# Weight conversion in a fused recurrence and feed-forward kernel: raw words fetched one unit ahead, conversion queued behind copies, masks and products, three prefix sums moved

## The chip, the core and the metric

The kernel runs on one core of one Trainium2 chip. The metric is the device time of one execution in microseconds (us). Every number below comes from the kernel's profile, from its trace or from the list of its times. The engines are named as the profile names them: PE is the matrix engine, PEld its weight loads, DVE the vector engine, ACT the scalar engine, POOL the general one, and SP the engine whose queue issues most transfers. Each engine works through its own list of instructions in order.

## The reference

Two blocks run one after the other. The first is a gated linear recurrence over 768 positions for 4 batches and 8 heads of width 48; the second is a product of two linear maps, followed by two more linear maps.

```python
# q, k, v, alpha: (4, 8, 768, 48) float32
for t in range(S):
    state = alpha[:, :, t, :, None] * state + np.einsum('bhd,bhe->bhde', k[:, :, t], v[:, :, t])
    y[:, :, t] = np.einsum('bhd,bhde->bhe', q[:, :, t], state)
x = y.transpose(0, 2, 1, 3).reshape(3072, 384)
a = x @ w1            # 384 x 1024, handed over as float64
b = x @ w2            # 384 x 1024
h = (a * b) @ w3      # 1024 x 1024
out = h @ w_out       # 1024 x 384
```

## The kernel before, in words

**Two parts share the engines.** Part one is the recurrence. It is cut into 24 steps (`N = 24`), each a chunk of 128 positions of one batch; six chunks make a batch. Part two is the feed-forward. Its matrix products run on float32 split into pieces (`h`, `l`, `m`), which is why one product of a 128x384 block takes nine matmuls for a contraction of 384 (L420: six in `products` with parts 0 and 1, then three with part 2). The products of `w1` and `w2` with `x` are called gates. They start inside part one, as filler, as soon as a group of three chunks has been written out and read back transposed.

**One step n of the loop at L599** traces its work in this order:

- the stores of the output chunk of two steps ago and the loads of chunks ahead, all on the SP queue (`store`, `load_v`, `load_a`, `load_kq`);
- `attend_state(n-1)` (L384 on PE: the state's share of the output), `scores(n)` (L364 on PE, then two masks `ms`, L367 on DVE), `transposed(n+1)` (L324 on PE, then two copies `qkT`, L326 on ACT);
- in every fourth step from 6 on `split_x` (L412 on ACT, L413 and L414 on DVE), which cuts a group of three chunks into pieces for the gates;
- a first piece of weight conversion (L627);
- `advance` (the decayed state, POOL), `attend(n-1)` (L390 on PE and the copies `x`, L394 on ACT), `outer(n)` (L336 on PE, then `T` on DVE), `third` (L232 and L233 on PE, L234 on ACT), a piece of gate work (`run`);
- a second piece of conversion (L636), `decayed(n+2)` (L302 on DVE: the products `qk` of keys and queries with the exponentials `e`), `logs(n+4)` (L271 on ACT: the logarithm `la` of a loaded alpha chunk `ac`), a third piece of conversion (L642), gate work, `decays(n+3)` (the prefix sum of `la` on PE, L286, or L289 from chunk 10 on, then two exponentials `e` on ACT, L292 and L293), a last piece of conversion (L646), gate work.

**Conversion** turns the float64 weights into float32 with bit operations. The weights `w1` and `w2` make twelve units of 128x512 values. A unit is a generator. Its first call issues the load of its raw 64-bit words (L192). After that it has four steps:

- step 1: ACT `rest` (L200), DVE `mant` and `power` (L201, L204), ACT `power` (L205);
- step 2: DVE L207, L208 and L210;
- step 3: ACT `w` (L217);
- step 4: DVE L219, and L221 for units 6 to 11. Units 0 to 5 leave that piece to `third` instead.

Units 0 to 5 make the first half of the gate weights, which all gates started in part one need. Units 6 to 11 are needed by the gates that follow part one. `convert(steps, ahead)` advances the oldest unit that has begun, one step per count, and before each step it issues loads until `ahead` units have begun. The pool of raw words has four buffers, `mant` three, `rest` and `power` two each.

**The order of instructions** is the tracing order only as a priority. The compiler's list scheduler places an instruction on its engine as early as it believes the inputs and buffers are there. An unmarked piece of conversion can so land in an engine's list several steps ahead of where it was traced. `after_marks(names)` opens a block in which every instruction traced on the engine of a marked instruction is listed behind it on that engine. It has no effect on other engines: `("qkT", n)` marks an ACT copy, `("ms", n)`, `("qk", n)` and `"x3"` mark DVE instructions.

**The decay of a carried state** crosses chunks in pairs. For an even chunk n inside a batch three rows (the last `e` of chunk n-1, the first `e` and the first alpha of chunk n) go to memory (L278, L295, L297, issued on POOL), come back as single values per partition (L310), and are multiplied into the state (L353 to L355) before `attend_state(n)`, which is traced in step n+1.

**After part one** only products, the conversion of `w3` and `w_out`, and the projections are left.

Of the kernel before, what the change touches and what calls it, by code (L numbers as in the profile page):

```python
# [48 lines left out]
def kernel(  # L49
# [18 lines left out]
    N = B * NCH  # L68
# [34 lines left out]
    def bank():  # L103
        return ps.tile([C, 512], FP32, tag="bank", name="bank")
# [3 lines left out]
    def after_marks(*names):  # L108
        stack = ExitStack()
        for x in names:  # L110
            stack.enter_context(tc.issue_after(mark[x]))
        return stack
# [16 lines left out]
    def load_a(n):  # L129
        if n < N:  # L130
            st["a", n] = inp.tile([C, H, D], FP32, tag="ac", name="ac")
            nc.sync.dma_start(out=st["a", n], in_=rows(alpha, n))  # L132

    def load_kq(n):
        if n >= N:
            return
        st["kq", n] = inp.tile([C, 2, H, D], FP32, tag="kq", name="kq")
        nc.sync.dma_start(out=st["kq", n][:, 0], in_=rows(k, n))  # L138
        nc.sync.dma_start(out=st["kq", n][:, 1], in_=rows(q, n))  # L139

    def load_v(n):
        if n < N:
            st["v", n] = vs[n % len(vs)]
            nc.sync.dma_start(out=st["v", n][:, :, 0:D], in_=rows(v, n))
# [91 lines left out]
    def fetch(ahead=3):  # L236
        while weights and len(begun) < ahead:
            begun.append(weights.popleft())
            next(begun[-1])

    def convert(steps, ahead=3):

        for _ in range(steps):
            fetch(ahead)
            if not begun:
                return
            x = begun.popleft()
            try:
                next(x)
                begun.appendleft(x)  # L250
            except StopIteration:
                pass
# [4 lines left out]
    def store():  # L257

        while later:
            dst, src = later.popleft()  # L260
            nc.sync.dma_start(out=dst, in_=src)
# [18 lines left out]
    def decays(n):  # L280
        if n >= N:
            return
        lc = bank()[:, 0:DM]
        la = st.pop(("la", n))
        if n < LATE:
            nc.tensor.matmul(lc, sums[:, n % 2].bitcast(FP32), la, start=True, stop=True)  # L286
        else:
            for i in range(2):
                nc.tensor.matmul(lc, sums[:, n % 2], la[:, i], start=(i == 0), stop=(i == 1))  # L289

        e = st["e", n] = work.tile([C, 2, DM], FP32, tag="e", name="e", bufs=3)
        nc.scalar.activation(e[:, 0], lc, AF.Exp, scale=-1.0)  # L292
        mark["e", n] = nc.scalar.activation(e[:, 1], lc, AF.Exp).ins  # L293
        if n in ends:
            nc.gpsimd.dma_start(out=ends[n][0:1], in_=e[0:1, 0])  # L295
        if n + 1 in ends:
            nc.gpsimd.dma_start(out=ends[n + 1][1:2], in_=e[C - 1:C, 1])  # L297
        load_ends(n)
# [6 lines left out]
    def load_ends(n):  # L305
        if n not in ends:
            return
        with nc.allow_non_contiguous_dma(reason="single values to partitions"):
            for i in range(2):
                nc.gpsimd.dma_start(out=decs[n // 2 % 2][ds(DP * i, D)].rearrange("d m j -> d (m j)"),  # L310
                                    in_=ends[n].rearrange("m (j i d) -> i d (m j)", i=2, d=D)[i])

    def transposed(n):
        if n >= N:
            return
        qk = qks[n % 3]
        qkT = work.tile([C, 2, NP, C], FP32, tag="qkT", name="qkT")

        tp = [bank().rearrange("p (i j c) -> p i j c", i=2, j=NP) for _ in range(2)]
        for i in range(2):  # L320
            for j in range(NP):
                for half in range(2):
                    s = ds(DP * half, DP)
                    nc.tensor.transpose(tp[half][:, i, j, :], qk[s, i, 2 * j:2 * j + 2, :], ident[s, s])  # L324
        for half in range(2):
            mark["qkT", n] = nc.scalar.copy(qkT[:, :, :, ds(DP * half, DP)], tp[half]).ins  # L326
        st["qkT", n] = qkT
# [30 lines left out]
    def scores(n):  # L358
        qkT = st["qkT", n]
        sc = [bank().rearrange("p (j c) -> p j c", j=NP) for _ in range(2)]  # L360
        for j in range(NP):
            for i in range(2):
                r = ds(DP * i, D)
                nc.tensor.matmul(sc[i][:, j, :], qkT[r, 0, j, :], qkT[r, 1, j, :], start=True, stop=True)  # L364
        ms = work.tile([C, 2, NP, C], FP32, tag="ms", name="ms")
        for i in range(2):
            masked = nc.vector.tensor_tensor(ms[:, i].bitcast(I32), sc[i].bitcast(I32), keep_bc, op=ALU.bitwise_and)  # L367
        ends_of_part1[0] = mark["ms", n] = masked.ins
        st["ms", n] = ms
# [3 lines left out]
    def attend_state(n):  # L373
        qkT = st.pop(("qkT", n))

        y = [bank()[:, 0:HP * C].rearrange("p (j c) -> p j c", c=C) for _ in range(2)]
        st["y", n] = y, [(half * HP + j, i, y[i][ds(DP * half, DP), j, :])
                         for j in range(HP) for i in range(2) for half in range(2)]  # L380
        if n % NCH:
            for j, i, to in st["y", n][1]:
                r = ds(DP * i, D)
                nc.tensor.matmul(to, Ts[n % 2][r, j, :], qkT[r, 1, j, :],  # L384
                                 start=(j % HP == 0), stop=False, skip_group_check=True)
# [18 lines left out]
    def load_x(g, queue=nc.sync):  # L404
        st["xT", g] = xp.tile([C, KM, TG], FP32, tag="xT", name="xT")
        queue.dma_start(out=st["xT", g], in_=xd[g].rearrange("(k p) t -> p k t", p=C))

    def split_x(g, i):
        x = st.pop(("xT", g))
        t = tr[i].tile([C, 3, KM, TG], FP32R, tag="x3", name="x3")  # L410
        st["x3", g] = t
        nc.scalar.activation(t[:, 0], x, AF.Copy, scale=1.0 - 2.0 ** -13)  # L412
        nc.vector.tensor_sub(t[:, 1], x, t[:, 0].bitcast(FP32))  # L413
        mark["x3"] = nc.vector.scalar_tensor_tensor(t[:, 2], t[:, 0].bitcast(FP32), -1.0 - 1.0 / P, x,  # L414
                                                    op0=ALU.mult, op1=ALU.add).ins
# [73 lines left out]
    def gate(g, f):  # L489
        yield from (late_gate if late else early_gate)(g, f)  # L490
# [105 lines left out]
    begin = {4 + 4 * g: (g, range(FH if g < 4 else KF)) for g in range(5)}  # L596
    loads = {8: 1, 11: 2, 15: 3, 19: 4}

    for n in range(N + 1):  # L599
        store()  # L600
        if n in loads:
            load_x(loads[n])
        load_v(n + AHEAD - 1)
        load_a(n + 5)
        load_kq(n + AHEAD)
        if n:
            attend_state(n - 1)
        if n < N:
            scores(n)
        transposed(n + 1)  # L610
        if n - 2 in begin:
            g, tiles = begin[n - 2]
            with after_marks(("ms", n), ("qkT", n + 1)):
                split_x(g, 0)
            fill.extend(gate(g, f) for f in tiles)
        pieces = (0, 3, 3, 2)[(n - 6) % 4] if n > 5 else 0
        if n == 0:
            with after_marks(("qkT", 0)):
                logs(2)
            decays(2)  # L620
            with after_marks(("e", 2)):
                logs(3)
        early, ready = n < 7, len(thirds)
        behind = after_marks(*[("qkT", n + 1), ("qk", n + 1)] * early, *["x3"] * (n - 2 in begin))
        if n < N - 2:
            with behind:
                convert(2 if n == 0 else 1, 2 if n == 0 else 3)  # L627
        advance(n)
        if n:
            attend(n - 1)  # L630
        outer(n)
        third(ready)
        run(pieces > 0)
        if early:
            with after_marks(("qkT", n + 1), ("qk", n + 1)):
                convert(1)  # L636
        with after_marks(*[("ms", n)] * (n < 3)):
            decayed(n + 2)
        logs(n + 4)
        if n == 4:  # L640
            load_x(0)
        convert(early and n > 2)  # L642
        run(pieces > 1)
        decays(n + 3)
        if n < N - 2:
            convert(early or n % 3 == 0)  # L646
        run(pieces > 2)
        if n == N - 3:
            while begun:
                convert(1)  # L650
            weights.extend(load_out(j) for j in range(KF))
            fetch(4)
# [91 lines left out]
```

## Time and profile before

The median of three runs is 481.35 us (479.03 to 481.43). The profiled execution has a span of 478.1 us.

| engine | busy us | share of the span | instructions |
|---|---|---|---|
| PE (matmul) | 457.8 | 96% | 3836 |
| PEld (weight load) | 434.0 | 91% | 3836 |
| DVE | 355.7 | 74% | 576 |
| ACT | 281.3 | 59% | 556 |
| POOL | 72.7 | 15% | 140 |

| what was moved | value |
|---|---|
| all transfers | 80.29 MB, mean 168 GB/s |
| packets under 512 B | 104480 of 153583 |
| a raw unit (L192) | 512 KB, 5.4 us from issue to landing |
| an alpha chunk (L132) | 192 KB, 5.0 us from issue to landing |

A busy share is an average over stages with different limits. Matmuls overlap in the PE, and the ends of their records are modelled, so a busy PE is not PE at its peak. The instructive reading is by stage: how long the same sequence of matmuls takes in one step and in another, and what released the engine that came last. A wait for several events is put down by the profile to the one that came last.

### The profile page before, as it was taken

The page shows a single profiled execution, that of the slowest core. Times are in us where ns is not written, and L with a number is a line of the kernel's source. Part 1 is how long each engine was busy: PE and PEld are TensorE (multiplying, and loading weights), DVE is VectorE, ACT ScalarE, POOL GpSimd, SP SyncE. Part 2 cuts the span into 40 slices and gives each one's busy share as a digit, 9 for nine tenths or more (in the row PEclk, how much of TensorE's full clock was granted, in tenths as well). Part 3 has the DMA queues.
Part 4 walks back from the last instruction along what each step waited for, and adds up shares of the span by engine and source line. Part 5 has one row for each costly group of instructions (what it writes and reads, how often), then busy time and mean ns, then how long its engine had stood idle before and what let it go on. Part 6 is the DMA issues. An engine that isn't in the chain of part 4 may idle for free.

```text
span 478.1 us, 9994 instructions
## 1 busy us (share of the span) xinstructions
PE 457.8 (96%) x3836; PEld 434.0 (91%) x3836; DVE 355.7 (74%) x576; ACT 281.3 (59%) x556; POOL 72.7 (15%) x140
## 2 busy tenths in 40 slices
PE   4879899999899999999999999999999999999996
PEld 2568689888899989999999999999999999999996
DVE  2669999886877977999998788745642876666761
ACT  4567877764757555898776666645544533333330
POOL 3311222112201310212331102112010100000000
PEclk9888999999899999999999999999999999999999
DMA  9999998999899974557775342122105965555511
GB/s 169 187 199 213 260 200 207 217 205 232 180 233 210 200 218 120 194 183 226 232 228 181 131 138 100 42 92 84 49 34 149 261 188 171 163 171 177 176 51 49
DMA packets 153583, 80.29 MB, mean 168 GB/s; under 512 B 104480, under 2 KB 145568, under 8 KB 153536
## 3 DMA queue, kind: packets, MB, share of 16 engines
q1 hardware_dynamic: 148016, 65.22, 56.4%
q0 software_dynamic: 5520, 14.43, 9.2%
q8 instruction: 30, 0.49, 0.5%
q14 instruction: 17, 0.14, 0.1%
HBM read 57.58 MB, written 22.06 MB: 167 GB/s over the span
## 4 chain that ended last, share of the span: by engine, by line
PE 82%; DMA 7%; SPq 4%; DVE 3%; ACT 2%; issue 1%; DVEq 0%; ACTq 0%
PE bank L420 68%; DMA raw<-in_moe_w_dram 5%; PE bank L390 4%; PE bank L364 3%; DMA ac<-in_alpha_dram 2%; SPq L139 2%; PE bank L324 2%; PE bank L384 2%; PE bank L522 1%; PE bank L336 1%; SPq L138 1%; PE bank L289 1%; SPq L132 1%; DVE qk L302 1%; ACT rest L200 0%
## 5 line engine op out<-in xcount | busy, mean ns | idle before, releaser
L420 PE MATMUL bank<-x,w 128*128 128x384 f32 x1152 | 211.1, 338 | 0.0
L420 PEld LDWEIGHTS bank<-x,w 128*128 128x128 f32 x1152 | 200.0, 188 | 1.9 <-issue 0.7
L420 PE MATMUL bank<-w3o,ab 128*128 128x384 f32 x576 | 100.2, 336 | 0.0
L420 PEld LDWEIGHTS bank<-w3o,ab 128*128 128x128 f32 x576 | 99.9, 188 | 0.0
L445 ACT ACTIVATE bank<-bank 128x384 f32<-128x384 f32 x98 | 46.7, 477 | 43.0 <-PE bank L420 42.6
L429 ACT ACTIVATE t<-bank 128x384 f32<-128x384 f32 x62 | 30.2, 493 | 57.5 <-PE bank L420 57.3
L495 POOL DMA_DIRECT2D abd<-ab x46 | 26.8, 583 | 132.7 <-DVE ab L481 124.9
L481 DVE TENSOR_TENSOR ab<-bank,r 128x384 f32<-128x384 f32 x45 | 24.9, 554 | 23.2 <-ACT bank L445 18.2
L551 DVE TENSOR_TENSOR ab<-abl,ab 128x1024 fp32r<-128x1024 f32 x24 | 29.4, 1224 | 14.0 <-ACT ab L550 14.0
L550 ACT ACTIVATE ab<-abl 128x1024 fp32r<-128x1024 f32 x24 | 25.5, 1061 | 20.9 <-PE bank L420 19.2
L420 PE MATMUL bank<-wo,w3T 128*128 128x384 f32 x192 | 35.9, 334 | 0.0
L367 DVE TENSOR_TENSOR ms<-bank,keep 128x512 int32<-128x512 int32 x48 | 31.5, 683 | 4.0 <-PE bank L364 4.0
L364 PEld LDWEIGHTS bank<-qkT 48*128 48x128 f32 x384 | 25.7, 202 | 9.2 <-ACT qkT L326 4.0
L420 PEld LDWEIGHTS bank<-wo,w3T 128*128 128x128 f32 x192 | 33.5, 188 | 0.0
L364 PE MATMUL bank<-qkT 48*128 48x128 f32 x384 | 30.7, 303 | 2.8 <-ACT qkT L326 2.5
L326 ACT COPY qkT<-bank 128x512 f32<-128x512 f32 x48 | 26.0, 589 | 11.8 <-PE bank L324 11.8
L431 DVE SCALAR_TENSOR_TENSOR o<-bank,t 128x384 f32<-128x384 f32 x24 | 13.4, 558 | 23.6 <-issue 14.9
L200 ACT ACTIVATE rest<-raw 128x512 f32<-128x512 uint32 (+1 forms) x36 | 23.1, 646 | 12.6 <-DMA raw<-in_moe_w_dram 11.8
L205 ACT ACTIVATE power<-power,rebias 128x512 uint32<-128x512 uint32 (+1 forms) x36 | 25.0, 697 | 9.5 <-DVE power L204 9.2
L302 DVE TENSOR_TENSOR qk<-kq,e 128x768 f32<-128x768 f32 x24 | 23.0, 958 | 9.3 <-ACT e L293 8.4
L552 DVE SCALAR_TENSOR_TENSOR ab<-ab,abl 128x1024 fp32r<-128x1024 f32 x24 | 29.2, 1218 | 0.0
L390 PE MATMUL bank<-ms,v 128*64 128x128 f32 x384 | 27.8, 290 | 0.0
(80 smaller groups left out, 570.7 us busy)
## 6 DMA issues: line engine op xcount, KB each, us to landing
raw<-in_moe_w_dram SPq DMA_DIRECT2D x28, 512.0 KB, 5.4
abl<-abd SPq DMA_DIRECT2D x24, 512.0 KB, 4.7
abd<-ab POOLq DMA_DIRECT2D x46, 192.0 KB, 3.2
xT<-xd POOLq DMA_DIRECT2D x9, 576.0 KB, 4.5
ac<-in_alpha_dram SPq DMA_DIRECT2D x24, 192.0 KB, 5.0
kq<-in_k_dram SPq DMA_DIRECT2D x24, 192.0 KB, 5.4
kq<-in_q_dram SPq DMA_DIRECT2D x24, 192.0 KB, 4.4
v<-in_v_dram SPq DMA_DIRECT2D x24, 192.0 KB, 4.9
```

The source lines that it names most:

```text
L302: mark["qk", n] = nc.vector.tensor_mul(qks[n % 3][:, :, :, 0:D], st.pop(("kq", n)), st.pop(("e", n)).rearrange("p i (h d) -> p i h d", h=H ...
L326: mark["qkT", n] = nc.scalar.copy(qkT[:, :, :, ds(DP * half, DP)], tp[half]).ins
L364: nc.tensor.matmul(sc[i][:, j, :], qkT[r, 0, j, :], qkT[r, 1, j, :], start=True, stop=True)
L367: masked = nc.vector.tensor_tensor(ms[:, i].bitcast(I32), sc[i].bitcast(I32), keep_bc, op=ALU.bitwise_and)
L390: nc.tensor.matmul(to, vc[:, 2 * j + i, :], ms[:, i, j, :], start=(n % NCH == 0 and j % HP == 0), stop=(j % HP == HP - 1), skip_group_chec ...
L420: nc.tensor.matmul(p, w[part][i], x[part][i], start=start and part == parts[0] and i == 0, stop=stop and part == parts[-1] and i == n - 1, ...
L429: nc.scalar.activation(t, p1, AF.Copy, scale=(1.0 + 1.0 / P) * scale)
L445: nc.scalar.activation(p, p, AF.Copy, scale=1.0 + 1.0 / P)
L495: (nc.gpsimd if late else nc.sync).dma_start(out=abd[g][:, f, :], in_=ab)
L550: nc.scalar.activation(t[:, 0], ab, AF.Copy, scale=1.0 - 2.0 ** -13)
L551: nc.vector.tensor_sub(t[:, 1], ab, t[:, 0].bitcast(FP32))
L552: nc.vector.scalar_tensor_tensor(t[:, 2], t[:, 0].bitcast(FP32), -1.0 - 1.0 / P, ab, op0=ALU.mult, op1=ALU.add)
```

## The change

It alters only the loop of part one. Conversion steps that were traced without a mark in steps 0 to 6 are merged into the two marked calls, and these calls are now marked behind the masks of the step (`("ms", n)`) as well as behind the copies of chunk n+1 and its products. From step 7 on the first call is marked behind the copies `qkT` of chunk n+1. The number of units that may have begun rises from 3 to 4 from step 8 on, so that a raw unit is asked for about a unit earlier. The prefix sums of chunks 3, 4 and 5 (`decays`) move from the end of steps 0, 1 and 2 to steps 1, 2 and 3, behind that step's scores and transposes. Step 0 advances conversion by three steps where it advanced it by four. The total amount of work is the same.

```diff
@@ -621,10 +621,12 @@
             with after_marks(("e", 2)):
                 logs(3)
         early, ready = n < 7, len(thirds)
-        behind = after_marks(*[("qkT", n + 1), ("qk", n + 1)] * early, *["x3"] * (n - 2 in begin))
+        behind = [("qkT", n + 1)] * (n < N - 1) + [("qk", n + 1), ("ms", n)] * early + ["x3"] * (n - 2 in begin)
+        if n in (1, 2, 3):
+            decays(n + 2)
         if n < N - 2:
-            with behind:
-                convert(2 if n == 0 else 1, 2 if n == 0 else 3)
+            with after_marks(*behind):
+                convert(1 + early, 2 if n == 0 else 3 if n < 8 else 4)
         advance(n)
         if n:
             attend(n - 1)
@@ -632,18 +634,18 @@
         third(ready)
         run(pieces > 0)
         if early:
-            with after_marks(("qkT", n + 1), ("qk", n + 1)):
-                convert(1)
+            with after_marks(*behind):
+                convert(1 + (n > 2))
         with after_marks(*[("ms", n)] * (n < 3)):
             decayed(n + 2)
         logs(n + 4)
         if n == 4:
             load_x(0)
-        convert(early and n > 2)
         run(pieces > 1)
-        decays(n + 3)
+        if n > 2:
+            decays(n + 3)
         if n < N - 2:
-            convert(early or n % 3 == 0)
+            convert(not early and n % 3 == 0, 3 if n < 8 else 4)
         run(pieces > 2)
         if n == N - 3:
             while begun:
```

## The prediction, made before the changed kernel was run

> **What bounds the kernel now.** I read the page's head and slices first, then the chain of waits, then busy time by stage, then the timeline at the places where the stages differ.
>
> ```profile
> span 478.1 us, 9994 instructions
> PE 457.8 (96%) x3836; PEld 434.0 (91%) x3836; DVE 355.7 (74%) x576; ACT 281.3 (59%) x556; POOL 72.7 (15%) x140
> PE   4879899999899999999999999999999999999996
> DVE  2669999886877977999998788745642876666761
> ```
>
> PE is full from about the fourth slice, apart from two 8s, and DVE is full for some slices early on. The chain says the same: from 123.45 us to 474.43 us it is PE alone. Time gained or lost before 123 us therefore moves the end one for one, and what comes later is a fixed remainder. The third view is busy time by stage (columns: stretch, its length, busy us and instructions of each engine, granted PE clock, DMA share, GB/s).
>
> ```profile
> 24.00:30.00 6.00, 6.00 (x90) 4.42 (x90) 1.56 (x4) 2.21 (x6) 1.37 (x4) 1.00 0.85 218
> 30.00:36.00 6.00, 3.46 (x48) 2.71 (x44) 6.00 (x13) 5.59 (x12) 1.07 (x2) 0.72 0.96 180
> 36.00:61.00 25.00, 23.41 (x339) 18.36 (x338) 23.28 (x41) 21.05 (x43) 4.47 (x9) 0.93 1.04 234
> 84.00:118.00 34.00, 33.71 (x456) 30.20 (x458) 27.37 (x46) 22.11 (x50) 5.66 (x12) 1.00 1.02 217
> 118.00:126.00 8.00, 5.78 (x83) 5.07 (x84) 5.15 (x8) 5.89 (x12) 1.41 (x2) 0.79 0.94 207
> 126.00:188.00 62.00, 62.00 (x791) 57.12 (x789) 50.34 (x88) 35.81 (x81) 11.44 (x20) 1.00 0.88 199
> ```
>
> Two places stand out. Around 24 to 36 us first DVE is idle (1.56 of 6 us busy), then PE (3.46 of 6). At 118 to 126 us PE loses time in the middle of its full stretch. The same view, taken over one identical sequence of matmuls (L384, L364, L324, L390, L336), gives its size: the steps that start at 96.98, 76.80 and 117.92 us.
>
> ```profile
> 96.98:101.51 4.53, 4.24 (x81) 3.73 (x81) 3.83 (x9) 3.50 (x9) 0.48 (x1) 1.00 1.20 210
> 76.80:80.46 3.66, 3.66 (x82) 3.37 (x81) 3.66 (x9) 1.75 (x5) 1.24 (x2) 1.00 0.87 173
> 117.92:125.52 7.60, 5.38 (x81) 4.67 (x80) 4.67 (x7) 5.89 (x12) 1.41 (x2) 0.78 0.92 206
> ```
>
> Undisturbed the sequence takes 3.66 us. At 117.92 it takes 7.60, so 3.94 us are lost; at 96.98 it takes 4.53, so 0.87 are lost. The timelines show by whom.
>
> ```profile
> 112.29 1.01 SPq L192 DMA_DIRECT2D raw<-in_moe_w_dram  x1
> ...
> 118.96 0.66 ACT L200 ACTIVATE rest<-raw 128x512 f32<-128x512 uint32 x1 [3.50 <-DMA raw<-in_moe_w_dram]
> 119.52 1.06 ACT L326 COPY qkT<-bank 128x512 f32<-128x512 f32 x2
> 120.63 1.44 PE L364 MATMUL bank<-qkT 48*128 48x128 f32 x16 [2.05 <-ACT qkT L326]
> ```
>
> The conversion read L200 stands in ACT's list ahead of the copies `qkT`, waits 3.50 us for raw words that were asked for at 112.29, and PE waits for the copies behind it. By count this is the eleventh unit (unit 10), traced in step 18 and listed in step 14. The same happens in miniature at 96.64 us with unit 9 (1.47 us). Early on:
>
> ```profile
> 18.45 1.17 PE L286 MATMUL bank<-la,sums 128*128 128x384 f32 x2 [2.27 <-ACT la L271]
> ...
> 26.98 0.69 DVE L367 TENSOR_TENSOR ms<-bank,keep 128x512 int32<-128x512 int32 x1 [2.30 <-PE bank L364]
> ...
> 28.01 0.53 POOL L295 DMA_DIRECT2D ends<-e  x1
> ...
> 29.81 0.68 ACT L200 ACTIVATE rest<-raw 128x512 f32<-128x512 uint32 x1 [2.42 <-DMA raw<-in_moe_w_dram]
> ...
> 34.93 1.41 POOL L310 DMA_DIRECT2D dec<-ends  x2 [6.39 <-DMA ends<-e]
> ```
>
> PE waits 2.27 us with the sum of chunk 3 ahead of the scores of chunk 1. ACT and DVE then both stand before unit 1's raw words until 29.81, and DVE is busy without a break from there.
>
> **What the Trainium skill says.** "Perfetto Trace Analysis", section "Sequencer Loop": an engine instruction waits in its engine's queue for its semaphores. The trace agrees: the copies start at 119.52, right behind the waiting L200, though their transposes had ended by 115.96. "DMA: Bandwidth & Descriptors", section "Anatomy of one DMA": the DMA engines wait for no semaphore, the issuing sequencer does, before dispatch. The trace agrees in kind: the load at L138 occupies the SP queue from 27.20 for 3.76 us, and the raw load traced behind it is issued at 31.93. "TensorE: Matmul & The Clock Gate", section "Part 1: The HAM clock gate": idleness of about 3.4 us halves the PE clock, and some 3.4 us of work restore it. The trace agrees on the effect, with an idle of only 2.05 us: the sixteen score matmuls take 1.44 us against 1.16, the sixteen of L390 1.76 against 1.09, at a granted clock of 0.78.
>
> **The change part by part.**
>
> *Raw words a unit sooner, from step 8.* Unit 9 is asked for in step 8 instead of 9, unit 10 in step 9 instead of 12, unit 11 in step 12 instead of 15. By the SP timeline, that puts unit 10 at about 91.3 us (where unit 9 stood) instead of 112.3, landing at about 96.7. Unit 10 cannot be read long before, because its `mant` buffer is unit 7's, which L221 of unit 7 frees. L217 ahead of that is now held behind the copies in step 11, at about 94 us. Unit 11 needs unit 8's buffer, free in step 14 or 15, when its words have been there for some us (112.3 plus 5.4). So the wait at 118.96 goes, and with it 3.94 us, of which 2.23 is idle PE and the rest slow PE. Unit 9's `rest` buffer is unit 7's, freed by L207 behind `x3` of step 10, about 92.5 us, and its words land at about 84.1 + 5.4 = 89.5: the 0.87 us at 96.98 go too. Sum: 4.8 us.
>
> *The price of that.* 512 KB come one step earlier, between 84 and 92 us: at 217 GB/s 2.4 us of transfer ahead of the alpha and key loads of that step. ACT already waits 2.13 us for alpha at 92.51. PE has 27 gate matmuls (5.1 us) there, but ACT also empties their banks. Bounds 0 and 2.4, I take 0.5 lost, since PE lost nothing behind the present 2.13.
>
> *Conversion behind copies, masks and products.* In steps 0 to 6 no instruction is added, only order changes. From 29.81 to 84 us DVE is busy almost throughout (6.00 of 6, 23.28 of 25, and 22.75 of 23 in the next stretch), so reordering inside that does not shorten it; it helps only where DVE was idle before 29.81. One conversion step fewer in step 0 moves 0.6 us of DVE (L219) by one step, into idle time: nothing. From step 7 on holding L217 behind the copies costs nothing, since units 6 to 11 are not needed before 188 us.
>
> *Sums of chunks 3 to 5.* With the sum of chunk 3 behind the scores of chunk 1, those can start when L336 ends (16.2 us) instead of 19.54. That lets DVE do the second mask of chunk 2, the `T` copy and the products of chunk 4 (0.60 + 0.27 + 0.87 = 1.7 us by start-to-start times) in its idle time, if the schedule lets them go ahead of the waiting conversion. Gain: 0 to 2.6 us (the upper end adds 0.9 us of PE wait at 31.02). Against it: `e` of chunk 4 moves behind the scores of step 2. If it lands behind L200 it comes at about 32.2 us instead of 26.5 (29.81 + 0.6 for L200 + two copies, 1.1, + one more ACT instruction of 0.7). Its row goes to memory and back: L295 at 28.01, L310 at 34.93, T at 42.38 to 42.89, wanted by L384 of step 5 at 45.33. Slack 2.4, delay 5.7: up to 3.3 us of PE wait. Between +2.6 and -3.3 I take +0.5.
>
> Sum: 4.8 - 0.5 + 0.5 = 4.8 us, 481.35 - 4.8 = 476.5.
>
> **The rivals.**
>
> *The early hole closes too.* DVE's two idle stretches (2.30 and 2.14) vanish, on top of 4.8 and about 1 us from PE's waits for logs near 65.8: 4.4 + 4.8 + 1.0 = 10.2, 471.2 us. Against it: unit 1's raw words are asked for no sooner, and transfers run at a share of 1.04 in 36 to 61 us.
>
> *The wait only moves.* The scheduler hoists the read as far as the load was moved, as units 9 and 10 show (each is read about two steps after its request), and unit 9's read meets step 10, which has no gate work to cover it. The 3.9 us reappear there: 481. For it: the hoisting. Against it: buffers hold the reads back.
>
> *Slower.* The decay row of chunk 4 comes late (3.3 us), the extra transfer delays alpha in a full stretch (2.4), unit 9 stalls step 10 (2.3), and only 3.9 us come back: 485.5 us.
>
> **How the numbers follow.** The forecast 0.50, the early hole 0.13, the moved wait 0.20, slower 0.17. The half per cent is 2.4 us. Faster takes forecast and early hole, and a little of the moved wait: 0.65. Same 0.18, slower 0.17. The range goes from just below the early rival, 470.5, to 484.0, leaving half of the slow case and a tenth of the early one outside.
>
> **What would show it.** Right: no ACT wait for raw above 1 us after 90 us; the five-line sequence of step 15 in about 3.7 us and the clock at 1.00 there; PE unbroken to the end. Step 1's scores near 17 us; T of chunk 4 ready before its L384. Wrong: L200 waiting in step 10 or 11 for unit 9; PE idle before L384 of step 5; alpha waits on ACT near 90 us that reach PE; the first gate matmul later than 61.23 us.

## The result, and the profile after

The changed kernel takes 486.99 us (median of six runs, 485.14 to 490.17) beside 480.9 us for the kernel before. The ratio is 1.014, with a 95% interval from 1.0098 to 1.0183. It is slower, and the time lies above the forecast range of 470.5 to 484.0. The profiled execution is the fastest of the six (485.14 us).

The head and two slice rows of the page of the changed kernel:

```profile
span 483.3 us, 9995 instructions
PE 457.9 (95%) x3836; PEld 434.6 (90%) x3836; DVE 356.9 (74%) x576; ACT 281.2 (58%) x556; POOL 74.0 (15%) x140
PE   4898729999999999999999999999999999999996
DVE  2678678899997957999999688846541966667771
```

The busy times are those of before (457.8 us on PE, 355.7 on DVE), so no work was added. The PE row has a new hole, 7 and 2 in the fifth and sixth slice, and after it only nines up to the last slice. The 8 in the eleventh slice, which the prediction wanted to remove, is gone. The view of busy time by stage sizes the hole (stretch, length, busy us and instructions of PE, PEld, DVE, ACT and POOL, granted PE clock, DMA share, GB/s):

```profile
46.00:58.00 12.00, 9.63 (x144) 7.15 (x143) 8.58 (x16) 9.98 (x22) 2.94 (x5) 1.00 0.94 207
58.00:71.00 13.00, 4.16 (x58) 3.42 (x56) 9.33 (x15) 6.03 (x12) 2.67 (x5) 0.72 0.96 212
71.00:78.00 7.00, 7.00 (x46) 6.58 (x45) 4.87 (x11) 5.67 (x13) 0.49 (x1) 0.78 0.97 229
78.00:128.00 50.00, 50.00 (x669) 45.66 (x671) 45.52 (x81) 35.14 (x80) 9.04 (x17) 1.00 1.06 216
```

From 58 to 71 us PE works for 4.16 of 13 us. From 78 us on it has no gap. The timeline of all engines in the hole shows what PE waits for:

```profile
62.12 1.16 ACT L412 ACTIVATE x<-xT 128x1152 fp32r<-128x1152 f32 x1 [0.63 <-DMA xT<-xd]
63.32 1.36 DVE L413 TENSOR_TENSOR x<-xT,x 128x1152 fp32r<-128x1152 f32 x1 [2.64 <-ACT x L412]
64.59 1.66 DVE L414 SCALAR_TENSOR_TENSOR x<-x,xT 128x1152 fp32r<-128x1152 f32 x1
66.18 0.68 DVE L207 SCALAR_TENSOR_TENSOR mant<-mant,rest 128x512 f32<-128x512 uint32 x1
...
67.72 0.68 DVE L210 TENSOR_TENSOR mant<-mant,power 128x512 f32<-128x512 f32 x1
68.43 0.63 ACT L217 ACTIVATE w<-mant 128x512 fp32r<-128x512 f32 x1 [2.65 <-DVE mant L210]
...
69.11 0.79 PE L232 MATMUL bank<-w,signs 128*128 128x512 f32 x1 [8.84 <-ACT w L217]
...
70.45 4.98 PE L420 MATMUL bank<-x,w 128*128 128x384 f32 x18
```

The same stretch in the first profile of the kernel before:

```profile
53.63 0.54 SPq L406 DMA_DIRECT2D xT<-xd  x1
54.21 0.49 SPq L192 DMA_DIRECT2D raw<-in_moe_w_dram  x1
...
55.38 0.68 DVE L210 TENSOR_TENSOR mant<-mant,power 128x512 f32<-128x512 f32 x1
...
56.93 0.69 DVE L219 SCALAR_TENSOR_TENSOR w<-w,mant 128x512 fp32r<-128x512 f32 x1 [0.61 <-ACT w L217]
...
58.45 1.17 ACT L412 ACTIVATE x<-xT 128x1152 fp32r<-128x1152 f32 x1 [0.19 <-DMA xT<-xd]
...
61.23 3.54 PE L420 MATMUL bank<-x,w 128*128 128x384 f32 x18
```

In the changed kernel DVE stands idle for 2.64 us before the split of `x` (L413), which waits for ACT's part of it and so for the transfer `xT`. Only behind the split come L207 to L210. They are step 2 of unit 5, the last unit of the first half of the gate weights. Its later pieces (L217, then `third` on PE) follow, and the first gate begins at 70.45 us. Before the change unit 5 was done (L219 at 56.93) ahead of the split, and the first gate began at 61.23, which is 9.22 us earlier. A second profile of the kernel before (e8, below) has it at 64.57.

The chain of waits adds the second cause, in order of time:

```profile
53.14 1.06 SPq L192
...
54.30 7.80 DMA xT<-xd
...
62.12 1.17 ACT x L412
```

The raw words of unit 6 (L192, 512 KB) now stand on the SP queue ahead of the read-back `xT`, which then takes 7.80 us to land. In the kernel before `xT` was issued first, at 53.63 us, and landed after 4.8. In the changed kernel the ACT instruction that reads it starts 3.7 us later (62.12 against 58.45).

What the prediction wanted in the middle did happen. The same sequence of five lines that took 7.60 us in step 15 before takes 4.01 us (columns as above):

```profile
126.54:130.55 4.01, 4.01 (x81) 3.55 (x81) 4.01 (x6) 3.98 (x11) 1.41 (x2) 1.00 1.06 184
```

The table puts these readings side by side for all kernels that were run, from the PE timelines: start of the first gate matmul, start of the scores of steps 8 and 23, and the time between the last two. From the scores of step 23 to the end every kernel needs 298.6 to 299.0 us, so all differences arise ahead of it. A position comes from one execution: seven profiles have the same code up to step 6 (before, e4, e5, e8, e9, e10, e12), and their first gates lie between 60.36 and 65.04 us. The changed kernel (70.45) and e6 (68.87) lie well outside that spread, e2 (65.83) just outside.

| kernel | first gate | step 8 | step 23 | between | median us | ratio to before (95%) |
|---|---|---|---|---|---|---|
| before, first profile | 61.23 | 68.49 | 179.30 | 110.81 | 480.9 | |
| before, second profile (e8) | 64.57 | 71.60 | 179.14 | 107.54 | | |
| changed | 70.45 | 77.91 | 184.35 | 106.44 | 486.99 | 1.014 (1.0098 to 1.0183) |
| e1, unit 5 free of the split | 63.43 | 72.78 | 181.48 | 108.70 | 481.94 | 1.003 (1.001 to 1.005) |
| e2, xT ahead of the raw words | 65.83 | 73.16 | 181.02 | 107.86 | 482.62 | 1.0056 (1.0036 to 1.0076) |
| e3, both | 62.33 | 69.50 | 177.93 | 108.43 | 480.56 | 0.999 (0.9972 to 1.0008) |
| e4, four units begun, alone | 61.49 | 69.50 | 179.22 | 109.72 | 479.84 | 0.9989 (0.9972 to 1.0005) |
| e5, late half alone | 61.25 | 69.60 | 178.23 | 108.63 | 477.99 | 0.9989 (0.9975 to 1.0004) |
| e6, early half alone | 68.87 | 75.97 | 184.04 | 108.07 | 484.37 | 1.0125 (1.0087 to 1.0163) |
| e7, sums alone | 63.38 | 70.49 | 178.73 | 108.24 | 478.77 | 0.9991 (0.9969 to 1.0014) |
| e9, before, fewer v loads | 60.36 | 67.95 | 175.01 | 107.06 | 475.98 | 0.9933 (0.9908 to 0.9958) |
| e10, late half, fewer v loads | 61.96 | 69.40 | 175.28 | 105.88 | 475.3 | 0.9914 (0.9888 to 0.9941) |
| e11, raw words later | 61.05 | 68.89 | 179.79 | 110.90 | 480.5 | 1.003 (1.0015 to 1.0046) |
| e12, v loads on POOL's queue | 65.04 | 72.10 | 181.92 | 109.82 | 482.17 | 1.0037 (1.0012 to 1.0063) |

Apart from the changed kernel itself, the medians come from four groups of runs, each with its own runs of the kernel before: 480.53 us beside e1 to e4, 478.75 beside e5 to e8, 478.79 beside e9 to e11, 480.03 beside e12. Only ratios can be compared across groups.

### The profile page after: what moved, and what is told of

It reads as the page before. It is cut to its first block, busy times and chain, and to the rows that moved or that the text cites. A ratio compares the mean times of both kernels' runs of the same rounds, so it can differ in the third digit from the quotient of the medians.

```text
span 483.3 us, 9995 instructions
## 1 busy us (share of the span) xinstructions
PE 457.9 (95%) x3836; PEld 434.6 (90%) x3836; DVE 356.9 (74%) x576; ACT 281.2 (58%) x556; POOL 74.0 (15%) x140
## 4 chain that ended last, share of the span: by engine, by line
PE 86%; DMA 5%; SPq 3%; DVE 2%; ACT 2%; issue 1%; ACTq 0%; DVEq 0%
PE bank L420 70%; PE bank L390 4%; PE bank L364 4%; DMA raw<-in_moe_w_dram 2%; PE bank L384 2%; PE bank L324 2%; DMA xT<-xd 2%; SPq L139 1%; PE bank L522 1%; PE bank L336 1%; PE bank L289 1%; DMA ac<-in_alpha_dram 1%; SPq L138 1%; SPq L132 1%; SPq L192 0%
## 5 line engine op out<-in xcount | busy, mean ns | idle before, releaser
L431 DVE SCALAR_TENSOR_TENSOR o<-bank,t 128x384 f32<-128x384 f32 x24 | 13.4, 557 | 23.7 <-issue 15.2
L431 DVE SCALAR_TENSOR_TENSOR r<-bank,t 128x384 f32<-128x384 f32 x38 | 21.0, 552 | 12.3 <-ACT t L429 8.6
L364 PEld LDWEIGHTS bank<-qkT 48*128 48x128 f32 x384 | 24.4, 193 | 5.5 <-issue 3.3
L364 PE MATMUL bank<-qkT 48*128 48x128 f32 x384 | 29.1, 291 | 0.0
L200 ACT ACTIVATE rest<-raw 128x512 f32<-128x512 uint32 (+1 forms) x36 | 23.3, 650 | 8.9 <-DMA raw<-in_moe_w_dram 8.9
```

Of the source, the lines that this page charges most:

```text
L431: nc.vector.scalar_tensor_tensor(to, p2, scale, t, op0=ALU.mult, op1=ALU.add)
```

## Experiments on the late gate

**e1: the conversion of step 6 free of the split.** On the changed kernel:

```diff
-        behind = ... + ["x3"] * (n - 2 in begin)
+        behind = ... + ["x3"] * (n - 2 in begin and not early)
```

> The changed kernel, with the mark x3 taken out of the conversion of step 6 only (it stays in steps 10, 14, 18 and 22). Theory (in the changed kernel steps 2 and 4 of unit 5 stand on DVE behind the split of x, which waits for its transfer, and the first gate waits for unit 5): unit 5 is done before the split; the first gate matmul comes when the split's second instruction ends, at about 65 us instead of 70.5, and the time falls by 5.5 us from 487.0, to 481.5, a ratio to before of 1.001. Rival A (unit 5 is late because step 0 advances one conversion step less and the rest follows): the gate stays at 70 us, 487, ratio 1.013. Rival B (the split of x sets the gate anyway, its transfer being late): gain 1 to 2 us only, 485.5, ratio 1.010.

It took 481.94 us, ratio 1.003, where the theory said 481.5 and the rivals 487 and 485.5. The PE timeline of this run, at its first gates:

```profile
63.43 0.79 PE L420 MATMUL bank<-x,w 128*128 128x384 f32 x3 [0.89 <-ACT x L412]
65.10 0.80 PE L420 MATMUL bank<-x,w 128*128 128x384 f32 x3 [0.88 <-DVE x L413]
66.46 3.89 PE L420 MATMUL bank<-x,w 128*128 128x384 f32 x12 [0.56 <-DVE x L414]
```

Unit 5 is ready here, and the gates come in the rhythm in which the split of `x` delivers its three pieces. What is left in this profile is the late transfer (`xT` landed 6.1 us after its issue, again behind the raw words).

**e2: xT ahead of the raw words.** On the changed kernel, in step 4:

```diff
+        if n == 4:
+            load_x(0)
         if n < N - 2:
             with after_marks(*behind):
                 convert(1 + early, 2 if n == 0 else 3 if n < 8 else 4)
...
-        if n == 4:
-            load_x(0)
```

> The changed kernel, with the read-back of the first group of x (xT, in step 4) traced ahead of that step's conversion, so that on the SP queue it goes ahead of the raw words of unit 6 and not behind them; the mark x3 stays. Theory (the raw words, 512 KB, stand ahead of xT and delay it): xT lands about 3 us sooner, near 59 us, split and unit 5 follow, first gate near 67.5 us, 484 us, ratio 1.006. Rival (the landing of xT is late because all transfers are slower there, whatever the order): it lands at 61 to 62 us, gate at 70, 487, ratio 1.013.

`xT` lands 4.3 us after its issue, and its ACT instruction starts at 58.56 us. That is 3.6 us earlier than in the changed kernel, from the order of the two transfers alone. The time is 482.62 us, ratio 1.0056. The other cause remains visible in the PE timeline:

```profile
65.24 0.80 PE L232 MATMUL bank<-w,signs 128*128 128x512 f32 x1 [4.79 <-ACT w L217]
```

**e3: both edits.**

> Both edits of the two kernels before on the changed kernel. Theory: the first gate comes near 61.5 us, as before the change, and what is left of the change is the wait for unit 10 taken away (3.9 us) and the smaller one for unit 9 (0.9 us): 476.5 to 477.5 us, ratio 0.992. Rival (the steps from 7 on went well only because the late gate left the transfers time to run ahead): the waits for raw words come back, 481, ratio 1.000.

The first gate is back at 62.33 us, and the loss is gone: 480.56 us, ratio 0.999. So the two causes together explain the loss, within the intervals. From the ratio of 1.014, e1 takes away 1.1% (about 5 us), e2 0.8% (about 4) and both 1.5% (about 7). The edits are not additive, since both causes lie on one chain: transfer, split, unit 5, gate. But the gain that the theory promised on top, a ratio of 0.992, is not there. The rival named the right time for a wrong reason: ACT had no wait for raw words at all between 70 and 135 us, and from step 8 to step 23 its waits for transfers of any kind sum to 0.3 us. What PE lost there was a few tenths of a microsecond at a time, behind DVE. The profiled execution is a fast one, 478.45 us beside the median of 480.56, so it need not show what a usual one loses. That sent the question to the middle of part one.

## Experiments on the middle of part one

**e4: only four units begun, on the kernel before.**

```diff
-                convert(2 if n == 0 else 1, 2 if n == 0 else 3)
+                convert(2 if n == 0 else 1, 2 if n == 0 else 3 if n < 8 else 4)
...
-            convert(early or n % 3 == 0)
+            convert(early or n % 3 == 0, 3 if n < 8 else 4)
```

> The kernel before, with only the fetch of raw words changed: four units may have begun from step 8 on. No mark, no moved sum. Theory (it is the moved request that takes the wait at 119 us away; the copies' marks matter little): the 3.9 us at 118 to 126 us are gone, unit 9 or 10 waits on ACT for at most 1.5 us in a step with gate work; 477 us, ratio 0.992. Rival (without the marks the read of raw words is hoisted as far as the request): PE loses 2 to 4 us at another step, 480 to 481, ratio 0.999.

The ratio is 0.9989 (0.9972 to 1.0005), as the rival said. The wait at 119 us is gone, and others stand in its place, the largest on PE in step 11. It is 1.33 us and so smaller than the rival's 2 to 4, and it stands behind a store of `x` and not behind a read of raw words. In all PE is idle for 2.8 us between the scores of steps 8 and 23, against 2.5 in the first profile of the kernel before. Timeline of this run, ACT and PE:

```profile
91.84 0.70 ACT L200 ACTIVATE rest<-raw 128x512 f32<-128x512 uint32 x1 [0.92 <-DMA raw<-in_moe_w_dram]
93.61 0.65 ACT L394 COPY x<-bank 128x256 f32<-128x256 f32 x2 [1.07 <-DMA xd<-x]
...
94.04 3.73 PE L420 MATMUL bank<-x,w 128*128 128x384 f32 x18 [1.33 <-ACT x L394]
```

**e5: the late half alone.** The edit of e4 on the kernel before, and the copies' mark from step 7 on:

```diff
-        behind = after_marks(*[("qkT", n + 1), ("qk", n + 1)] * early, *["x3"] * (n - 2 in begin))
+        behind = after_marks(*[("qkT", n + 1)] * (n < N - 1), *[("qk", n + 1)] * early, *["x3"] * (n - 2 in begin))
```

> The kernel before with only the late half of the change: from step 7 on the marked conversion call stands behind the copies qkT, and four units may have begun from step 8 on. Steps 0 to 6 and the sums are as before. Theory (the late half does what the prediction said, and all that is lost is lost in steps 4 to 6): first gate near 61.3 us, no wait for raw words near 119 us, steps 8 to 23 in 106.4 to 108.5 us by the start of the scores (110.8 before, 106.4 in the changed kernel), 476.5 to 478.5 us, ratio 0.992 to 0.996. Rival (the middle went well in the changed kernel because its gates began late and let transfers and conversion run ahead): steps 8 to 23 in 110 us or more, ratio 1.000.

The first gate is at 61.25 us, and ACT waits for raw words nowhere between 70 and 135 us, as the theory said. The ratio is 0.9989 (0.9975 to 1.0004) all the same, where the theory had 0.992 to 0.996, and steps 8 to 23 take 108.63 us, just above the theory's range and well under the rival's 110. ACT's timeline shows other waits in its place, all for transfers:

```profile
92.58 0.65 ACT L394 COPY x<-bank 128x256 f32<-128x256 f32 x2 [1.65 <-DMA xd<-x]
...
110.73 0.52 ACT L271 ACTIVATE la<-ac 128x384 f32<-128x384 f32 x1 [2.40 <-DMA ac<-in_alpha_dram]
...
121.94 0.65 ACT L394 COPY x<-bank 128x256 f32<-128x256 f32 x2 [1.70 <-DMA xd<-x]
```

**e6: the early half alone.** The changed kernel with its late half put back:

```diff
-        behind = [("qkT", n + 1)] * (n < N - 1) + [("qk", n + 1), ("ms", n)] * early + ["x3"] * (n - 2 in begin)
+        behind = [("qkT", n + 1), ("qk", n + 1), ("ms", n)] * early + ["x3"] * (n - 2 in begin)
...
-                convert(1 + early, 2 if n == 0 else 3 if n < 8 else 4)
+                convert(1 + early, 2 if n == 0 else 3)
...
-            convert(not early and n % 3 == 0, 3 if n < 8 else 4)
+            convert(not early and n % 3 == 0)
```

> The changed kernel with its late half put back: from step 7 on the conversion call has no mark qkT and three units may have begun, as before; steps 0 to 6 and the sums are as in the changed kernel. Theory (late half worth about 4 us, early half a loss of about 9): first gate near 70.5 us, steps 8 to 23 in about 110.8 us as in the kernel before, 490 us, ratio 1.019. Rival (the late gate itself buys the smooth steps after it): first gate near 70.5 us, steps 8 to 23 in 106 to 107 us, 486.5 us, ratio 1.013.

The first gate is at 68.87 us and the ratio 1.0125 (1.0087 to 1.0163), which includes that of the whole change. Within the intervals the early half is the whole loss. The theory's 1.019 was wrong; the rival's 1.013 was right. Steps 8 to 23 take 108.07 us without the late half, nearer to the rival's 106 to 107 than to 110.8: the late half is not needed for a smooth middle.

**e7: the sums alone.** On the kernel before:

```diff
+        if n in (1, 2, 3):
+            decays(n + 2)
...
-        decays(n + 3)
+        if n > 2:
+            decays(n + 3)
```

> The kernel before with only the sums of chunks 3, 4 and 5 moved to steps 1, 2 and 3. Theory (from 30 us on DVE and the raw words set the pace, so an earlier start of the scores is not kept): scores of chunks 1 and 2 start 3 to 4 us sooner, the first gate within 1 us of 61.2, 480.5 us, ratio 0.998 to 1.002. Rival (the decay row of chunk 4 comes late and PE waits for the state in step 5): first gate 2 to 4 us later, 483 us, ratio 1.006.

No effect on the time: 0.9991 (0.9969 to 1.0014). The scores of chunk 1 start at 14.63 us and not at 19.54, those of chunk 2 at 25.68 against 25.79; the early start is lost within a step. The gate at 63.38 us misses the one microsecond of the theory, and lies between the two profiles of the kernel before. The rival's wait of PE for the state in step 5 did come, and was 1.50 us long:

```profile
46.30 0.67 PE L384 MATMUL bank<-qkT,T 48*64 48x128 f32 x16 [1.50 <-POOL T L355]
```

Here `e` of chunk 4 landed behind the waiting L200, at 32.13 us, where the prediction had put it for that case (32.2). The rival's loss of time, a ratio of 1.006, did not follow from it.

**e8: the kernel before, a second profile.**

> The kernel before, unchanged, profiled a second time. If the wait for raw words at 118 to 121 us belongs to the kernel, ACT waits there 3 to 4 us again and steps 8 to 23 take 110 to 111 us. If it was an accident of the first profile, the wait is below 1.5 us or at another step, and the gain forecast from it was read from one execution only.

The span is 477.9 us, against 478.1 in the first profile, and yet the inside is another (PE's and ACT's timelines of this execution):

```profile
64.57 3.30 PE L420 MATMUL bank<-x,w 128*128 128x384 f32 x18
...
117.87 0.70 ACT L200 ACTIVATE rest<-raw 128x512 f32<-128x512 uint32 x1 [0.94 <-DMA raw<-in_moe_w_dram]
```

The first gate is 3.3 us later, the wait for raw words is 0.94 us and not 3.50, and steps 8 to 23 take 107.54 us and not 110.81. In these two executions one and the same program lost its time in different places, once in the middle and once ahead of the first gate. The hole of 3.94 us that the forecast was built on was one side of such an exchange. That the two sides always balance is not shown: e12, the same program up to step 6, has both a late gate (65.04) and a long middle (109.82).

## Experiments on what sets the pace of the middle

First, PE's own work is a floor. Between the scores of steps 8 and 23 stand the same 1428 matmuls before and after the change, and where PE has no idle time among them, in the changed kernel and in e10, they take 106.44 and 105.88 us. So only some 5 us stood above the floor in the first profile of the kernel before (110.81), and under 2 in the second (107.54).

The candidate for what stands above it is the transfers: their share is near 1 in all stages up to about 168 us.

**e9 and e10: 192 KB fewer per step.** On the kernel before, and on e5:

```diff
-            nc.sync.dma_start(out=st["v", n][:, :, 0:D], in_=rows(v, n))
+            if n < 10:
+                nc.sync.dma_start(out=st["v", n][:, :, 0:D], in_=rows(v, n))
```

> The kernel before, with the loads of v left out from chunk 10 on (16 heads' rows of an older chunk are used again), so that 192 KB fewer are moved in each step from step 7 on; no other engine has less work. Theory now (in steps 7 to 16 the transfers set the pace, and a wait that is taken away shows up as a wait for another transfer): the waits for alpha, raw words and stored x after 70 us shrink, the start of step 23's scores moves from 178 to 179 us to 175 to 176 us, 476 to 477 us against 479 to 480.5 for the kernel before, ratio 0.992 to 0.995. Rival (the order of conversion on ACT and DVE sets the pace): no change, ratio 0.998 to 1.002.

> The late half of the change alone, with the same loads of v left out from chunk 10 on. Theory (transfers are the floor under the late half): with them lighter the late half shows its worth, steps 8 to 23 take 106.4 to 107 us at a first gate of 61 to 62 us, step 23's scores start near 175 us, 475 us, ratio 0.990. Rival (order of conversion): the same ratio as with v loaded, 0.999.

The scores of step 23 start at 175.01 and 175.28 us, as the theory said, and the ratios are 0.9933 and 0.9914. No engine has less to compute in these kernels, so in steps 7 to 20 the loads are worth about 3 us that the order of conversion is not. By which wait they cost it is open. In e9 the waits of ACT for transfers between the scores of steps 8 and 23 did not shrink, as the theory wanted: they sum to 9.5 us, as in the first profile of the kernel before. PE's idle time there did, from 2.5 to 0.9 us. The early gate of e9 (60.36) is not the edit's doing, since the first load left out would be issued at about 71 us. Whether the late half adds anything under lighter loads is not shown: the two intervals overlap.

**e11: raw words later, not sooner.** On the kernel before, none is fetched in steps 6 to 11:

```diff
-            with behind:
-                convert(2 if n == 0 else 1, 2 if n == 0 else 3)
+            with behind:                     # with the qkT mark of e5
+                if 12 <= n < 14:
+                    fetch(2)
+                else:
+                    convert(2 if n == 0 or n > 13 else 1, 1 if 7 < n < 12 else 2 if n == 0 or n > 5 else 3)
...
-            convert(early or n % 3 == 0)
+            convert(early or n == 9, 3 if n < 6 else 2 if n < 8 else 1)
```

The other two calls of steps 0 to 6 are limited to two begun units in step 6.

> The kernel before with the raw words of units 8 to 11 asked for later and not sooner: none is fetched in steps 6 to 11, units 8 and 9 in step 12, the others as those are done; units 8 to 11 are converted two steps per step of the loop from step 14 on, behind the copies qkT. Nothing is left out. Theory (transfers set the pace up to about 130 us and are slack after it): 1 MB less is moved between 69 and 112 us, worth up to 4.8 us at 217 GB/s; the waits there shrink, step 23's scores start at 175.5 to 177 us, 476.5 to 478 us against 479 to 480.5, ratio 0.993 to 0.997. Rival (raw words are not what competes, or the later conversion loads DVE in its turn): ratio 0.999 to 1.005.

The ratio is 1.003 (1.0015 to 1.0046): a miss. The first part came true. The scores of step 16 start at 127.65 us, against 131.35 and 129.34 in the two profiles of the kernel before. But then ACT waits longer for the alpha loads of later steps, which the raw words now accompany (ACT and PE timelines of this run):

```profile
139.36 0.52 ACT L271 ACTIVATE la<-ac 128x384 f32<-128x384 f32 x1 [2.67 <-DMA ac<-in_alpha_dram]
...
148.27 0.52 ACT L271 ACTIVATE la<-ac 128x384 f32<-128x384 f32 x1 [3.47 <-DMA ac<-in_alpha_dram]
...
149.81 1.16 PE L364 MATMUL bank<-qkT 48*128 48x128 f32 x16 [2.17 <-ACT qkT L326]
```

The assumption that transfers are slack after 130 us was wrong: their share between 130 and 180 us is 0.94 in the kernel before. Moving raw words within part one gained nothing either way (e4, e11). That it was the raw words that delayed these alpha loads is not shown: the second profile of the kernel before has a wait for alpha of 2.63 us at 136.87.

**e12: the same loads on another queue.**

```diff
-            nc.sync.dma_start(out=st["v", n][:, :, 0:D], in_=rows(v, n))
+            (nc.gpsimd if n > 9 else nc.sync).dma_start(out=st["v", n][:, :, 0:D], in_=rows(v, n))
```

> The kernel before, with the loads of v from chunk 10 on issued on POOL's queue and not on SP's. Nothing is left out: the bytes and pieces are the same, but SP has one issue less per step. Theory (the transfers themselves set the pace): no gain, ratio 0.998 to 1.004, step 23's scores at 178 to 180 us. Rival (SP's time for issuing is what paces the loads, and leaving the v loads out helped by relieving SP): ratio 0.992 to 0.996, step 23's scores at 175 to 176 us.

The ratio is 1.0037 (1.0012 to 1.0063). Taking these issues off SP gains nothing, so the rival's 0.992 to 0.996 is out. The scores of step 23 start at 181.92 us, later than the theory's 178 to 180, behind a first gate at 65.04. POOL is busier in exchange (31.7 us between the scores of steps 8 and 23, against 20.9), and what that costs was not measured. The likely reading is that the gain of e9 came from the transfers that were not made, and not from SP's time; a gain on SP that POOL's extra work cancels is not excluded. Whether bytes or the number of 192-byte pieces count was not tried.

No kernel that makes all the loads beats the one before by more than its interval; e4 and e5 come nearest, at 0.9989.

## Why the prediction was wrong

The sum was 4.8 - 0.5 + 0.5 us of gain; measured were 6.1 us of loss. By its own steps:

- **"In steps 0 to 6 no instruction is added, only order changes", costed at nothing inside DVE's busy stretch: this is the step that failed.** It read the marks for copies, masks and products and passed over the last name in the same list, `x3`, which it met only for step 10. In step 6 that mark puts everything in both marked calls on DVE behind the split of `x`. With one conversion step fewer behind it, unit 5 had step 2 still to do there; before the change that step was done in step 5, and the second call carried no such mark. A busy engine was taken for one on which order is free. But one instruction in its list waits for a transfer (2.64 us of idle DVE ahead of L413), and what is listed behind it waits too. e1 measures this at 1.1%, about 5 us. The same paragraph also put the step fewer in step 0 at nothing; it is what left step 2 of unit 5 for step 6. In e3 that step is missing as well and nothing is lost, so it did harm only together with the other two; a kernel with that step put back and the mark `x3` kept was not tried.
- **"Raw words a unit sooner, from step 8."** The limit on begun units does not change before step 8, but the place of the request does: merging two steps into the second call fetches unit 6 in step 4 ahead of `load_x(0)` and not behind it. The prediction put the price of sooner raw words at 84 to 92 us and never looked at step 4. This too is a matter of order in steps 0 to 6 that was costed at nothing. e2 measures it at 0.8%, about 4 us, on the same chain as e1. The statement that the first gate later than 61.23 us would show the forecast wrong pointed at the right place; no step led to it, and its threshold was too fine, since the kernel before has the gate at 64.57 itself.
- **The 4.8 us of the two holes.** The reading of the large hole was exact for the execution it came from, and the mechanism held: no wait for raw words above 1.01 us in the middle of the changed kernel, the five lines of step 15 in 4.01 us. In the small hole the copies `qkT` stood ahead of the waiting read (92.94 against 96.64 us), and PE waited 0.29 us, for DVE's L431. That the buffers hold the reads back is not shown: the changed kernel reads units 10 and 11 at 5.7 and 5.0 us after their requests, as soon as the words are there. The value was wrong. The late half is worth -0.1% (e5, interval -0.25 to +0.04%), about 0.5 us. The wait is 0.94 us in the second profile of the same kernel, and in e5, without it, other transfers make ACT wait. The rival "the wait only moves" had this in its title, with step 10 as the place; it moved instead to alpha loads and stores of `x` in steps 11 to 15, and it had 0.20.
- **The price of the extra transfer, 0.5 us**, was not measured by itself. It is contained in the result of the late half (e5).
- **The sums, between +2.6 and -3.3, taken as +0.5.** The scores of chunk 1 start at 16.25 us, as worked out (16.2). The gain was not kept: 0 within 0.2% (e7). The danger named, the decay row of chunk 4, did not arise in the changed kernel: `e` of chunk 4 stayed ahead of the waiting L200, and T was ready at 43.26 us for an L384 at 44.77. With the sums alone it did arise, at 1.50 us of PE's wait (e7).
- **The slower rival** (485.5 us, 0.17) named the side and nearly the time, but none of its three terms shows in the changed kernel: it blamed the decay row, alpha and step 10.

The loss is not the full 9.22 us by which the first gate is late. Steps 8 to 23 take 110.81 us in the first profile of the kernel before and 106.44 in the changed kernel, where PE is never idle among them. So 4.4 us of the delay are made up, and 5.1 reach the scores of step 23 (184.35 against 179.30). A likely reason is that the loads run ahead while PE stands still; no run isolates this.

## What to carry to other kernels

Before counting a wait as a gain, take a second profile of the same program, and ask what would set the pace if the wait were gone. Here PE's own work did, not far below, and in e4 and e5 a wait that was taken from one instruction came back at others, mostly for other transfers. When an edit moves work into a block with ordering marks, go through each name in the list and ask what the marked instruction itself waits for: a mark on an instruction that waits for a transfer makes all that the block lists behind it wait for that transfer. And look at which transfers change places on their queue when the code that issues them moves by a few lines.

## What the runs showed of the hardware that was not expected

A transfer of 576 KB (`xT`) took 4.3 to 5.8 us to land when no raw unit stood directly ahead of it on its queue (before, e2, e3, e5, e7, e8), and 6.1 to 7.8 us when a raw unit of 512 KB did (e1, e6, the changed kernel). After PE's 8.84 us without work the granted clock was 0.78 in the next 7 us, and the first eighteen gate matmuls took 4.98 us from the first start to the last end, against 3.54 in the kernel before.
